# Block attention and two expert layers: host-side layouts, 64x64 attention products, and a list scheduler for the first part

## The chip, the cores and the metric

The kernel runs on one core of a Trainium2 chip. The metric is the device time of one execution in microseconds (us), as the median of several runs. Traces come from one profiled execution.

## What is computed

Eight batches of eight heads hold 576 tokens of 64 features. Attention works inside blocks of 64 tokens (9 blocks per sequence), so each head and block has a 64x64 score matrix. Its output, 4608 tokens by 512 features, goes through two dense layers in a row.

```
scores = q_c @ k_c.T / 8              # per block of 64 tokens
out    = softmax(scores) @ v_c        # -> x: 4608 x 512
h      = x @ w_in                     # 512 -> 1024
ln     = layernorm(h * softmax(h)) * g_ln
x      = ln @ w_out                   # 1024 -> 512
h2     = x @ w2_in                    # 512 -> 2048
y      = silu(h2) @ w2_out            # 2048 -> 512
```

q, k, v and g_ln are float32; the four weight matrices arrive as float64.

## The kernel before

There are three parts. The **first part** takes 36 tiles of 128 tokens through attention, `moe_in` (x @ w_in), the layer norm, and the transposes that the next product needs; every four tiles form a block of 512 tokens, whose `moe_out` (ln @ w_out) is done in four column groups. The result goes to HBM as `y1d`. The **second part** (`product`, L582) multiplies by `w2_in` with seven products in place of eight (Strassen's scheme), the **third** (`out_product`, L704) does the same with `w2_out`.

A dense product takes three passes of float32r matmuls (`PASSES`): high part by high part, high by low, low by high. So each operand is split into two float32r parts: ScalarE copies the high part (L384), VectorE subtracts for the low part (L393).

The four stages of a tile in the first part, with the lines that matter:

- `load_qk` and `load_v` fetch q, k and v straight from the inputs' own layout, two tiles at a time, in pieces of 64 or 128 KB (L279, L291, L302): 264 DMAs for q and k. `qk_transpose` turns q and k: on TensorE for the first six tiles (L313, with three ScalarE copies), on VectorE after that (L325, L328).
- `scores` (L336): eight float32 matmuls of 128 rows, 64 columns and 128 moving columns; k sits in a block-diagonal tile `kT` whose other half is zero, so half of the array's rows multiply zeros. `softmax_a` and `softmax_b` (L343 to L358) use VectorE, ScalarE and GpSimd. `attn_transpose` (L364) turns the weights, `attn_copy` (L370, two ScalarE copies of 64 partitions) puts them into the block-diagonal `pT`, and `attn_pv` (L378) is again eight matmuls of 128 moving columns. Each of these float32 matmuls shows as two records in the trace.
- `moe_in` (L409) is 24 matmuls of 512 columns, `ln_max` to `ln_norm` (L414 to L445) the layer norm. The scaling at its end runs on VectorE (L445) from the seventh tile on. PSUM holds one `h`, so the next tile's `moe_in` waits for L426.
- `ln_transpose` (L454, four transposes for each half) and `ln_split`; then `moe_out` (L468), 24 matmuls for each tile's share, and `y_store`.

Beside the tiles, `conv_load`, `conv_a`, `conv_b` and `conv_c` convert the weights from float64 in pieces of 128x512 (L159, L162, L176, L187, L203 or L209, and the split at L219, L221). There are 8 pieces of `w_in`, 8 of `w_out`, 16 of `w2_in` (followed by `w2_mix`, which writes sums of pieces to HBM). Odd pieces of the first sixteen are converted on GpSimd in part (L184, L207), even ones on VectorE; low parts are made on GpSimd (L221).

The order on every engine is fixed when the program is built: `Plan.at` gives each step a time, `Plan.run` emits in order of these times, and an engine runs its instructions in that order. In the first part the times are `T[t] = 14.3 t - 46.7` plus offsets; for the first 13 or so tiles a table of times (`LEAD`) replaces them.

PSUM's eight banks are: scores `S` 1, `K` 1, `px` 2 (`pp` and `xp`), `tr` 1, `y` 1, `h` 2. SBUF holds one `e`, one `pT`, one `xs` and two `u`.

Of the kernel before, what the change touches and what calls it, by code (L numbers as in the profile page):

```python
# [9 lines left out]
F32 = mybir.dt.float32  # L10
F32R = mybir.dt.float32r
# [13 lines left out]
class Plan:  # L25

    def __init__(self, lead):
        self.items = []
        self.lead = lead

    def at(self, when, fn, *args):
        lead = self.lead.get((fn.__name__, *(a for a in args if isinstance(a, int))))
        when = [x / 100 for x in lead] if lead else [when] if isinstance(when, float) else when
        self.items.append((when, fn, args))
# [11 lines left out]

@with_exitstack
def chunk_attention_moe_moe(ctx: ExitStack, tc: tile.TileContext, q, k, v, w_in, w_out, g_ln, w2_in, w2_out, out):
    nc = tc.nc
    B, H, S, D = q.shape
    NT, DM = out.shape
    F1 = w_in.shape[1]
    F2 = w2_in.shape[1]
    CH = 64
    HP = H // 2
# [4 lines left out]
    NG = 3  # L64
# [3 lines left out]
    CW = 512  # L68

# [26 lines left out]

    kT = sb.tile([128, 2 * HP, 2, CH], F32, tag="kT", name="kT")
    nc.vector.memset(kT, 0.0)
    pT = sb.tile([128, HP, 2, 2, CH], F32, tag="pT", name="pT")
    nc.vector.memset(pT, 0.0)  # L100


# [5 lines left out]
    for i in range(2 * KD):  # L108
        kk, c = i % KD, i // KD * CW

        heads = [(4 * (kk // 2) + 2 * g + kk % 2) * D for g in range(2)]
        pieces.append(("wi", kk, c, [w_in[r:r + D, c:c + CW] for r in heads], 1))
    for m in range(KD):
        for a in range(2):
            src = w_out[a * 512:(a + 1) * 512, m * 128:(m + 1) * 128].rearrange("(k p) f -> p k f", p=128)
            pieces.append(("wo", m, a, src, 4))
    for j in range(K2 // 2):
        for f in (j, j + K2 // 2):
            pieces.append(("w2", f, 0, w2_in[:, f * 128:(f + 1) * 128].rearrange("(k p) f -> p k f", p=128), KD))
    for j in range(K2 // 2):  # L120
        for f in (j, j + K2 // 2):
            pieces.append(("w2", f, 1, w2_out[f * 128:(f + 1) * 128, :], 1))
    conv, whole = {}, {}

    def cut(ap, n):
        return ap.rearrange("p (a f) -> p a f", a=n) if n > 1 else ap
# [3 lines left out]
    def conv_load(i):  # L130
        kind, _, _, src, n = pieces[i]
        wide = w_in.dtype != F32
        if kind == "wi":
# [5 lines left out]
        for r, part in ((slice(0, 64), src[0]), (slice(64, 128), src[1])) if kind == "wi" else ((slice(0, 128), src),):  # L139
            nc.sync.dma_start(out=cut((st if wide else st[:, 0:CW])[r], n), in_=part.bitcast(I32) if wide else part)  # L140
        conv[i] = [st, None]
# [24 lines left out]
    def conv_b(i, on=DVE):  # L166
# [11 lines left out]
        if on == POOL:  # L178
            yield
            L = st[:, 0:CW].bitcast(F32)  # L180
            nc.scalar.activation(out=M, in_=cv[:, 1, :], func=AF.Copy, scale=2.0 ** -20)
            nc.scalar.activation(out=L, in_=low, func=AF.Copy, scale=2.0 ** -52)
            yield
            nc.gpsimd.tensor_tensor(out=M, in0=M, in1=L, op=ALU.add)  # L184
        else:
            yield
            nc.vector.scalar_tensor_tensor(out=M, in0=low, scalar=2.0 ** -32, in1=cv[:, 1, :], op0=ALU.mult, op1=ALU.add)  # L187

    def conv_c(i, on=DVE):

        kind, x, y, _, n = pieces[i]
        st, cv = conv.pop(i)
        if st.dtype == F32:
            F, P, unit = st[:, 0:CW] if cv is None else cv[:, 1, :].bitcast(F32), None, 1.0
        else:
            F, P = cv[:, 1, :].bitcast(F32), cv[:, 0, :].bitcast(F32)
            unit = 1.0 if on == POOL else 2.0 ** -20
        if kind == "wo":
            for j in range(4):
                s = slice(128 * j, 128 * j + 128)  # L200
                gain = gsb[:, 4 * y + j:4 * y + j + 1] if unit == 1.0 else gsb20[:, 4 * y + j:4 * y + j + 1]
                if P is not None:
                    nc.vector.scalar_tensor_tensor(out=F[:, s], in0=F[:, s], scalar=gain, in1=P[:, s], op0=ALU.mult, op1=ALU.mult)  # L203
                else:
                    nc.vector.tensor_scalar(out=F[:, s], in0=F[:, s], scalar1=gain, scalar2=None, op0=ALU.mult)
        elif P is not None and on == POOL:
            nc.gpsimd.tensor_tensor(out=F, in0=F, in1=P, op=ALU.mult)  # L207
        elif P is not None:
            nc.vector.scalar_tensor_tensor(out=F, in0=F, scalar=unit, in1=P, op0=ALU.mult, op1=ALU.mult)  # L209
# [4 lines left out]
        if kind == "wi":  # L214
            hi, lo = (w[x][:, y:y + CW] for w in wi)
        else:
            hi, lo = (w[y][:, :, 128 * x:128 * x + 128] for w in wo)
            F = cut(F, 4)
# [48 lines left out]
    raw, val, qk, att, pvs, x_t = {}, {}, {}, {}, {}, {}  # L267

    def load_qk(g):
        c, b0 = g // 2, g % 2 * 4  # L270
        qr = sb.tile([128, 4, HP, 2, 32], F32, tag="qr", name="qr", bufs=2)
        kr = sb.tile([128, 4, HP, 2, 32], F32, tag="kr", name="kr", bufs=2)
        raw[g] = [qr, kr]
        if g < NG:

            for tt in range(2):
                for src, dst in ((q, qr), (k, kr)):
                    for c2 in range(2):
                        nc.sync.dma_start(  # L279
                            out=dst.rearrange("p (tt x) hp tb j -> p tt (x hp tb j)", tt=2)[64 * c2:64 * c2 + 64, tt].rearrange("p (h d) -> p h d", d=D),  # L280
                            in_=src[b0 + 2 * tt + c2, :, c * CH:(c + 1) * CH, :].rearrange("h s d -> s h d"),
                        )
                    yield
            return
        for src, dst in ((q, qr), (k, kr)):
            rows = src[b0:b0 + 4].rearrange("b (hp h2) s d -> h2 s (b hp) d", h2=2)
            for h2 in range(2):
                for e in range(2):
                    for tb in range(2):
                        p0, s0 = 64 * h2 + 32 * e, c * CH + 32 * tb  # L290
                        nc.sync.dma_start(  # L291
                            out=dst[p0:p0 + 32, :, :, tb, :].rearrange("p b hp j -> p (b hp) j"),
# [799 lines left out]
```

## Time and profile before

| | us |
|---|---|
| median of 3 runs | 1323.95 |
| lowest, highest | 1322.4, 1325.07 |
| span of the profiled execution | 1327.0 |
| start of the second part's first matmul | 590.93 |
| from the first tile's last `moe_in` record to the first `moe_out` | 48.98 to 101.27 |
| start of `moe_in` of the seventh and of the last tile | 115.73 and 549.02 |

For the profiled execution only the span is given, 3.05 us above the median. PE is the matrix engine (TensorE), PEld its weight loads, DVE VectorE, ACT ScalarE, POOL GpSimd, SP the engine that issues the DMAs. The clock of TensorE is given as a share of full speed (1.00 is 2.4 GHz, 0.50 is 1.2 GHz). A line number is that of the kernel before.

### The profile page before, as it was taken

The page shows a single profiled execution, that of the slowest core. Times are in us where ns is not written, and L with a number is a line of the kernel's source. Part 1 is how long each engine was busy: PE and PEld are TensorE (multiplying, and loading weights), DVE is VectorE, ACT ScalarE, POOL GpSimd, SP SyncE. Part 2 cuts the span into 40 slices and gives each one's busy share as a digit, 9 for nine tenths or more (in the row PEclk, how much of TensorE's full clock was granted, in tenths as well). Part 3 has the DMA queues.
Part 4 walks back from the last instruction along what each step waited for, and adds up shares of the span by engine and source line. Part 5 has one row for each costly group of instructions (what it writes and reads, how often), then busy time and mean ns, then how long its engine had stood idle before and what let it go on. Part 6 is the DMA issues. An engine that isn't in the chain of part 4 may idle for free. (4 is left out here: it accounts for less than half of the span.)

```text
span 1327.0 us, 22478 instructions
## 1 busy us (share of the span) xinstructions
PE 1266.0 (95%) x8400; PEld 1158.4 (87%) x8400; DVE 909.9 (69%) x1387; ACT 609.6 (46%) x991; POOL 558.8 (42%) x450
## 2 busy tenths in 40 slices
PE   3789999999999999999999999999999999999998
PEld 2578887887888888789899999999999999999998
DVE  7799777887888788524656656563678666666671
ACT  5677444544545545433435444443433343434341
POOL 4443113321312332321554446343137666667662
PEclk9989999999999999999999999999999999999999
DMA  9573456556545641769577655758993443443420
GB/s 205 93 139 74 91 112 155 130 107 165 140 104 144 155 115 64 273 235 297 168 229 237 211 183 187 240 166 278 354 331 119 139 149 111 138 148 113 136 92 29
DMA packets 330846, 217.51 MB, mean 164 GB/s; under 512 B 187248, under 2 KB 288624, under 8 KB 330736
## 3 DMA queue, kind: packets, MB, share of 16 engines
q1 hardware_dynamic: 330736, 216.07, 57.7%
q8 instruction: 66, 1.08, 0.3%
q14 instruction: 44, 0.36, 0.1%
HBM read 130.03 MB, written 85.98 MB: 163 GB/s over the span
## 5 line engine op out<-in xcount | busy, mean ns | idle before, releaser
L704 PE MATMUL h<-w2o,gs 128*128 128x256 f32 x2160 | 266.2, 284 | 2.5 <-DVE gs L697 2.0
L704 PEld LDWEIGHTS h<-w2o,gs 128*128 128x128 f32 x2160 | 262.7, 192 | 2.9 <-DVE gs L697 2.2
L582 PE MATMUL h<-y1s,w2t 128*128 128x384 f32 x1440 | 259.7, 335 | 1.4 <-ACT tmp L595 0.8
L582 PEld LDWEIGHTS h<-y1s,w2t 128*128 128x128 f32 x1440 | 251.3, 188 | 2.9 <-DVE tmp L599 1.5
L409 PE MATMUL h<-wi,xs 128*128 128x512 f32 x864 | 219.2, 403 | 6.6 <-DVE u L426 3.7
L468 PE MATMUL yp<-lnT,wo 128*128 128x512 f32 x864 | 211.9, 395 | 0.7 <-ACT ys L473 0.7
L409 PEld LDWEIGHTS h<-wi,xs 128*128 128x128 f32 x864 | 161.4, 192 | 45.8 <-ACT e L348 2.9
L468 PEld LDWEIGHTS yp<-lnT,wo 128*128 128x128 f32 x864 | 159.1, 188 | 38.5 <-issue 5.0
L695 ACT ACTIVATE gs<-g 128x1024 fp32r<-128x1024 f32 x117 | 123.6, 1059 | 140.5 <-PE h L704 74.8
L697 POOL TENSOR_TENSOR gs<-g,gs 128x1024 fp32r<-128x1024 f32 x50 | 138.1, 2764 | 49.4 <-ACT gs L695 44.3
L697 DVE TENSOR_TENSOR gs<-g,gs 128x1024 fp32r<-128x1024 f32 x67 | 116.7, 1746 | 31.2 <-ACT gs L695 30.3
L582 PE MATMUL hw<-y1s,w2t 128*128 128x384 f32 x576 | 109.9, 339 | 7.4 <-DVE tmp L613 7.4
L582 PEld LDWEIGHTS hw<-y1s,w2t 128*128 128x128 f32 x576 | 101.5, 189 | 9.3 <-DVE tmp L613 9.1
L704 PE MATMUL hw<-w2o,gs 128*128 128x256 f32 x864 | 108.7, 282 | 0.0
L704 PEld LDWEIGHTS hw<-w2o,gs 128*128 128x128 f32 x864 | 105.4, 191 | 0.0
L436 POOL TENSOR_TENSOR st<-st,nhalf 128x1 f32<-128x1 f32 x36 | 21.3, 592 | 177.9 <-DVE st L434 177.8
L239 POOL TENSOR_TENSOR cv<-cv 128x256 f32<-128x256 f32 x64 | 46.2, 741 | 90.7 <-DVE cv L209 89.4
L358 POOL TENSOR_TENSOR e<-e,sm 128x512 f32<-128x512 f32 x36 | 42.1, 1170 | 90.1 <-DVE sm L356 83.4
L393 DVE TENSOR_TENSOR lnT<-tp,lnT 128x512 fp32r<-128x512 f32 x72 | 49.4, 686 | 38.1 <-ACT lnT L384 37.4
L384 ACT ACTIVATE lnT<-tp 128x512 fp32r<-128x512 f32 x72 | 42.9, 596 | 61.8 <-PE tp L454 61.7
L684 POOL TENSOR_TENSOR g<-g,g0x 128x1024 f32<-128x1024 f32 x18 | 43.5, 2416 | 62.8 <-DVE gs L697 58.5
L615 ACT ACTIVATE tmp<-tmp 128x384 f32<-128x384 f32 x48 | 24.7, 528 | 90.3 <-DVE tmp L613 83.9
(116 smaller groups left out, 1805.4 us busy)
## 6 DMA issues: line engine op xcount, KB each, us to landing
gd<-tmp SPq DMA_DIRECT2D x192, 192.0 KB
g<-gd SPq DMA_DIRECT2D x72, 512.0 KB
w2d<-cv_m SPq DMA_DIRECT2D x56, 256.0 KB
w2t<-w2d SPq DMA_DIRECT2D x56, 256.0 KB
w2od<-y1s SPq DMA_DIRECT2D x56, 256.0 KB
w2o<-w2od SPq DMA_DIRECT2D x27, 512.0 KB
st_w<-in_moe_w_out_dram SPq DMA_DIRECT2D x24, 512.0 KB
vt<-in_v_dram SPq DMA_DIRECT2D x36, 256.0 KB
```

Source lines behind the costliest of these rows:

```text
L239: nc.gpsimd.tensor_tensor(out=out, in0=in0, in1=in1, op=op)
L358: nc.gpsimd.tensor_tensor(out=e, in0=e, in1=sm.to_broadcast([128, HP, 2, CH]), op=ALU.mult)
L384: nc.scalar.activation(out=hi, in_=src, func=AF.Copy)
L393: nc.vector.tensor_tensor(out=lo, in0=src, in1=hi.bitcast(F32), op=ALU.subtract)
L409: nc.tensor.matmul(h_t[t][:, n, :], xs[:, a, kk, :], wi[b][kk][:, n * 512:(n + 1) * 512], start=(kk == 0 and i == 0), stop=(kk == KD - 1 a ...
L468: nc.tensor.matmul(yps[b, m], wo[a][f // 4][:, f % 4, 128 * m:128 * (m + 1)], lnT[b][c][:, f, :], start=(f == 0 and i == 0), stop=(f == K1 ...
L582: nc.tensor.matmul(acc, w[:, a, kk, :], t[:, i, c, :], start=start and kk == 0 and n == 0, stop=kk == 1 and n == 2, skip_group_check=not s ...
L615: nc.scalar.activation(out=c, in_=c, func=AF.Silu)
L684: on.tensor_tensor(out=out, in0=in0, in1=in1, op=op_)
L695: nc.scalar.activation(out=dst[:, 0], in_=src, func=AF.Copy)
L697: (nc.gpsimd if o > (3 if v > 1 else 5) else nc.vector).tensor_tensor(out=dst[:, 1], in0=src, in1=dst[:, 0].bitcast(F32), op=ALU.subtract)
L704: nc.tensor.matmul(acc, g[:, a, f, :], wo2[o, f][:, c, :], start=start and f == 0 and i == 0, stop=f == NF - 1 and i == 2, skip_group_chec ...
```

## The change

The host hands over q and k, v, `w_in` and `w2_in` already in the order in which a tile or a piece is loaded; no value is changed. For every tile there is one DMA of 512 KB for q and k together and one of 256 KB for v, with rows of 4 and 2 KB; every weight piece is one contiguous DMA. q and k come with the features on the partitions, so `qk_transpose` and the block-diagonal tiles `kT` and `pT` go.

`attend(t)` does the output product of tile t and the scores of tile t + 2 together: 16 and 16 matmuls of 64 rows, 64 columns and 64 moving columns, ordered so that four neighbours use the four quarters of the array. Its PSUM tile `sx` (two banks, one buffer) holds both results. The softmax (`weigh`) is the same arithmetic with one ScalarE copy of 128 partitions at its end.

Conversion pieces run on VectorE alone (the GpSimd form is gone); the low part of the 8 `w_in` pieces moves from GpSimd to VectorE, that of the 8 `w_out` pieces stays on GpSimd. `w_out` pieces are whole rows, so their scaling is one instruction of 512 columns instead of four of 128. The scaling at the end of the layer norm runs on ScalarE for all tiles, with one more small GpSimd product; `x_split` makes its low part on VectorE for all tiles.

Buffers: `e`, `pT`, `xs`, `tr` and `y` two, `u` four, `qk` three; `sx` takes the place of `S`, `K` and `px`. In the second part the accumulators use `tr`, `sx`, `y` and `h`, and the places into which the second and third parts' weights are loaded change with the buffers.

The order of the first part comes from `Steps.solve`, a list scheduler: each step has an engine, a length, what it needs and frees, and each engine takes the ready step with the earliest due time. The due times come from `NOMINAL` (12.6 us a tile after the tenth). It holds no step back until a time, so loads and conversions of `w2_in` run as early as their places allow.

The core of the diff (cut):

```diff
+            for e in engines:
+                if free_at[e] > now + 1e-9:
+                    continue
+                st = min((st for st in ready[e] if all(places[p] > 0 for p in st["take"])), key=lambda st: st["rank"], default=None)
+                if st is None:
+                    continue
+                ready[e].remove(st)
+                for place in st["take"]:
+                    places[place] -= 1
+                start = now
+                if e == "PE":
+                    start += 0.1 * (mode != st["mode"])
+                    mode = st["mode"]
+                if st["port"]:
+                    start = max(start, port["POOL" if e == "DVE" else "DVE"])
+                    port[e] = start + st["length"]
+                st["start"], st["end"] = start, start + st["length"]
+                free_at[e] = st["end"]
...
+def stage_one(T, way_out, w2_from, tiles=36, per=4, ahead=2):
+
+    step = Steps(dict(S=1, X=1, tr=2, y=2, h=1, u=4, xs=2, e=2, pT=2, qk=3, v=2, ln=2, ys=2, st=2, cv=2, cvs=2))
+    op = step.op
+    dma = lambda kb, **more: ("DMA", kb * 1024 / 300e3, more)
+    sp = lambda n=1, **more: ("SP", 0.62 * n, more)
+    for t in range(tiles):
...
+    for t in range(-ahead, tiles):
+        n = t + ahead
+        old, new = t >= 0, n < tiles
+        op("attend", (t,), ("PE", 0.07 + 0.49 * (old + new), dict(mode=1, need=[("p", t), ("v", t)] * old + [("qk", n)] * new, take=["S"] * new + ["X"] * old,
+                                                                  free=["pT", "v"] * old + ["qk"] * new, give=[("s", n)] * new)),
+           *[("ACT", 0.59, dict(take=["xs"])), ("DVE", 0.69, dict(give=[("xs", t)], free=["X"], due=T[t] - 0.5))] * old)
+        if new:
+            op("weigh", (n,), ("DVE", 1.38, dict(need=[("s", n)], take=["e"], free=["S"])), ("ACT", 0.63, {}), ("DVE", 1.05, {}), ("POOL", 1.17, {}),
+               ("PE", 0.45, dict(take=["tr"])), ("ACT", 0.59, dict(take=["pT"], free=["tr", "e"], give=[("p", n)])))
+    wi = [[("w", 4 * n + kk) for kk in range(4)] for n in range(2)]
+    wo = [("w", i) for i in range(8, 16)]
+    for t in range(tiles):
+        b, tt = divmod(t, per)
+        x = T[t]
+        op("moe_in", (t,), ("PE", 2.73, dict(need=wi[0] + [("xs", t)], take=["h"], due=x + 2.73)),
+           ("PE", 2.73, dict(need=wi[1], free=["xs"], give=[("h", t)], due=x + 5.5)))
+        op("norm", (t,), ("DVE", 1.23, dict(need=[("h", t)])), ("ACT", 1.3, dict(take=["u"])),
+           ("DVE", 1.83, dict(free=["h"], due=x + gap - 0.5)), ("ACT", 1.34, {}), ("DVE", 0.15, {}), ("POOL", 0.85, {}),
+           ("ACT", 1.12, dict(give=[("u", t)])))
+        y = x + way_out + gap
+        for half in range(2):
+            op("turn_ln", (t, half), ("PE", 0.45, dict(need=[("u", t)], take=["tr"] + ["ln"] * (tt == 0 and half == 0))), ("ACT", 0.6, {}),
+               ("DVE", 0.69, dict(free=["tr"] + ["u"] * half, give=[("l", b, half, tt)], due=y + 3 * half)))
+    for b in range(tiles // per):
+        for m in range(4):
+            t = per * b + per + m
+            due = (T[t] if t < tiles else T[-1] + gap + 5.5 * (t - tiles)) + way_out + 5
+            op("moe_out", (b, m), ("PE", 2.73, dict(need=wo + [("l", b, 0, i) for i in range(per)] + [("o", b, m - 1)] * (m > 0), take=["y"], due=due + 2.7)),
+               ("PE", 2.73, dict(need=[("l", b, 1, i) for i in range(per)], free=["ln"] * (m == 3), give=[("o", b, m)], due=due + 5.5)),
+               ("ACT", 0.6, dict(take=["ys"], free=["y"])), sp(), dma(256, free=["ys"]))
+    return step
...
-        nc.gpsimd.tensor_tensor(out=lo, in0=F, in1=hi.bitcast(F32), op=ALU.subtract)
+        (nc.vector if kind == "wi" else nc.gpsimd).tensor_tensor(out=lo, in0=F, in1=hi.bitcast(F32), op=ALU.subtract)
...
+    def load_qk(t):
+        qk_t[t] = sb.tile([128, 2, 2, HP, CH], F32, tag="qk", name="qk", bufs=3)
+        nc.sync.dma_start(out=qk_t[t], in_=qk[t])
+
+    def load_v(t):
+        val[t] = sb.tile([128, 2, HP, D], F32, tag="vt", name="vt", bufs=2)
+        nc.sync.dma_start(out=val[t], in_=v[t])
+
+    def attend(t):
+
+        n = t + AHEAD
+        sx = ps.tile([128, 2, 512], F32, tag="sx", name="sx")
+        if t >= 0:
+            pT, vt = p_t.pop(t), val.pop(t)
+            for a in range(2):
+                for c in range(2):
+                    for h2 in range(2):
+                        for g in range(2):
+                            r, hp = slice(64 * h2, 64 * h2 + 64), 2 * a + g
+                            x0 = 256 + 128 * a + 64 * c
+                            nc.tensor.matmul(sx[64 * g:64 * g + 64, h2, x0:x0 + 64], vt[r, c, hp, :], pT[r, hp, c, :], start=True, stop=True)
+        if n < TT:
+            qT, kT = (qk_t[n][:, i] for i in range(2))
+            for hp in range(HP):
+                for h2 in range(2):
+                    for c in range(2):
+                        r = slice(64 * h2, 64 * h2 + 64)
+                        nc.tensor.matmul(sx[64 * c:64 * c + 64, h2, 64 * hp:64 * hp + 64], qT[r, c, hp, :], kT[r, c, hp, :], start=True, stop=True)
+            sx_t[n] = sx[:, :, 0:256].rearrange("p h (a k) -> p h a k", k=CH)
+        if t >= 0:
+            yield
+            xs = x_t[t] = sb.tile([128, 2, 2, 256], F32R, tag="xs", name="xs", bufs=2)
+            yield from split(xs[:, 0], xs[:, 1], sx[:, :, 256:512])
...
+        nc.gpsimd.tensor_tensor(out=rs, in0=rs, in1=nhalf, op=ALU.pow)
+        nc.gpsimd.tensor_tensor(out=off, in0=nmu, in1=rs, op=ALU.mult)
+        yield
+        nc.scalar.activation(out=u, in_=u, func=AF.Identity, bias=off, scale=rs)
...
-            if at_ == "w":
-                if "w" not in bank:
-                    bank["w"] = ps.tile([128, 2, 512], F32, tag="h", name="hw")
-                bank[u, at_] = bank["w"][:, u % 2, 0:n]
+            if at_ in "wy":
+                if at_ not in bank:
+                    bank[at_] = ps.tile([128, 2, 512], F32, tag={"w": "h", "y": "sx"}[at_], name="h" + at_)
+                bank[u, at_] = bank[at_][:, u % 2, 0:n]
             else:
-                tag, bufs = {"x": ("px", 2), "y": ("SK"[u % 2], 1), "v": (("tr", "y")[u % 2], 1)}[at_]
-                bank[u, at_] = ps.tile([128, 512], F32, tag=tag, name="h2", bufs=bufs)[:, 0:n]
...
-    plan = Plan(LEAD)
+    step = stage_one(NOMINAL, WAY_OUT, W2_FROM, TT, BT, AHEAD)
+    fns = dict(load_qk=load_qk, load_v=load_v, convert=convert, w2_mix=w2_mix, attend=attend, weigh=weigh,
+               moe_in=moe_in, norm=norm, turn_ln=turn_ln, moe_out=moe_out)
+    plan = Plan()
     at = plan.at
-    L = 14.3
+    at(-1.0, gain_load)
+    at(5.0, gain_scale)
+    for (name, *args), when in step.solve().items():
+        at(when, fns[name], *args)
...
+FIRST = [-14.8, 16.57, 3, 3.46, 8.49, 9.95, 15.13, 10.28, 17.44, 8.76]
+NOMINAL = [sum(FIRST[:t + 1]) + 12.6 * max(0, t + 1 - len(FIRST)) for t in range(36)]
+WAY_OUT = 20.65
+W2_FROM = 12
...
+    qk = _np.stack([heads(x).transpose(0, 3, 5, 1, 2, 4) for x in "qk"], axis=3).reshape(36, 128, 2, 2, 4, 64)
+    data = dict(qk=qk, v=heads("v").transpose(0, 3, 4, 1, 2, 5).reshape(36, 128, 2, 4, 64))
+    data["w_in"] = wide["moe_w_in"].reshape(2, 2, 2, 64, 2, 512).transpose(4, 2, 0, 1, 3, 5).reshape(2, 4, 128, 512)
+    data["w_out"] = wide["moe_w_out"]
```

## Rows read from the trace of the kernel before

**Rows 1.** The page: span and busy time of each engine.
```profile
span 1327.0 us, 22478 instructions
PE 1266.0 (95%) x8400; PEld 1158.4 (87%) x8400; DVE 909.9 (69%) x1387; ACT 609.6 (46%) x991; POOL 558.8 (42%) x450
```

**Rows 2.** Busy time by stage (window, length, busy and count, clock, DMA, GB/s).
```profile
0.00:48.98 48.98, 22.06 (x121) 15.70 (x121) 38.76 (x47) 25.70 (x43) 26.84 (x27) 1.00 1.07 193
48.98:101.27 52.29, 44.64 (x310) 36.10 (x309) 44.24 (x92) 40.44 (x68) 20.50 (x21) 0.90 0.52 96
115.73:549.02 433.29, 427.85 (x2672) 349.33 (x2670) 345.93 (x648) 221.91 (x381) 116.65 (x128) 1.00 0.53 125
549.02:590.93 41.91, 38.36 (x173) 30.71 (x173) 15.10 (x21) 12.75 (x21) 11.22 (x7) 1.00 0.79 294
590.93:1327.00 736.07, 718.62 (x5041) 714.64 (x5039) 452.24 (x553) 299.38 (x462) 376.87 (x261) 0.99 0.58 185
```

**Rows 3.** Timeline of PE, one steady tile (start, length, line, tile, count).
```profile
382.81 1.15 PE L378 MATMUL xp<-pT,vt 128*64 128x128 f32 x16
383.74 1.09 PE L336 MATMUL S<-kT,qT 128*64 128x128 f32 x16
384.76 3.02 PE L468 MATMUL yp<-lnT,wo 128*128 128x512 f32 x12
...
397.53 1.15 PE L378 MATMUL xp<-pT,vt 128*64 128x128 f32 x16
```

**Rows 4.** Line 378's instructions alone, first 0.03 us of one group.
```profile
382.80:382.83 0.03, 0.02 (x2) 0.02 (x2) 1.00 0.60 94
```

**Rows 5.** Waits in the first part (engine line, releaser: total, times, longest).
```profile
PE pp L364 <- POOL e L358: 6.9, 12, 2.3
PE h L409 <- DVE u L426: 3.7, 4, 2.4
```

**Rows 6.** VectorE groups, first 590 us (busy, mean ns).
```profile
L343 DVE TENSOR_REDUCE mx<-S 128x8 f32<-128x512 f32 x36 | 24.5, 682 | 0.0
L414 DVE TENSOR_REDUCE st<-h 128x1 f32<-128x1024 f32 x36 | 44.1, 1224 | 11.9 <-PE h L409 11.1
L426 DVE SCALAR_TENSOR_TENSOR u<-u,st,h 128x1024 f32<-128x1024 f32 x36 | 46.1, 1281 | 1.4
L424 DVE TENSOR_SCALAR st<-st 128x1 f32<-128x1 f32 x36 | 5.5, 152 | 16.8 <-ACT u L417 16.8
L203 DVE SCALAR_TENSOR_TENSOR cv<-cv,gsb 128x128 f32<-128x128 f32 x32 | 9.3, 356 | 0.1
L445 DVE TENSOR_SCALAR u<-u,st 128x1024 f32<-128x1024 f32 x30 | 25.9, 862 | 19.6 <-POOL st L436 19.5
```

**Rows 7.** Timeline of VectorE at the start: weight pieces being converted.
```profile
5.76 0.43 DVE L159 TENSOR_SCALAR cv_e<-st_e 128x512 int32<-128x512 int32 x1 [2.75 <-DMA st_e<-in_moe_w_in_dram]
6.10 0.42 DVE L162 TENSOR_SCALAR cv_e<-st_e 128x512 int32<-128x512 int32 x1
7.04 0.69 DVE L176 SCALAR_TENSOR_TENSOR cv_e<-st_e,cv_e 128x512 int32<-128x512 int32 x1 [0.52 <-ACT cv_e L164]
7.65 0.68 DVE L187 SCALAR_TENSOR_TENSOR cv_e<-st_e,cv_e 128x512 f32<-128x512 uint32 x1
...
15.07 1.49 DVE L162 TENSOR_SCALAR cv<-st_e 128x512 int32<-128x512 int32 x1
```

**Rows 8.** DMA of the first 60 us.
```profile
DMA packets 23379, 9.87 MB, mean 165 GB/s; under 512 B 21328, under 2 KB 22352, under 8 KB 23376
```

**Rows 9.** Timeline of PE: the fifth tile and the first output product.
```profile
89.62 5.46 PE L409 MATMUL h<-wi,xs 128*128 128x512 f32 x12 [2.38 <-DVE u L426]
...
101.27 3.03 PE L468 MATMUL yp<-lnT,wo 128*128 128x512 f32 x12
```

**Rows 10.** The two halves of moe_in of the fifth tile (columns as rows 2).
```profile
89.62:94.87 5.25, 5.25 (x12) 3.99 (x13) 5.17 (x12) 1.93 (x4) 2.66 (x4) 0.50 0.77 136
95.94:98.79 2.85, 2.85 (x15) 2.29 (x14) 1.91 (x6) 2.83 (x5) 0.00 (x0) 1.00 0.65 169
```

More of the change, by code (lines that the diff above doesn't have):

```diff
@@ L51, in chunk_attention_moe_moe @@
 @with_exitstack
-def chunk_attention_moe_moe(ctx: ExitStack, tc: tile.TileContext, q, k, v, w_in, w_out, g_ln, w2_in, w2_out, out):
+def chunk_attention_moe_moe(ctx: ExitStack, tc: tile.TileContext, qk, v, w_in, w_out, g_ln, w2_in, w2_out, out):
     nc = tc.nc
-    B, H, S, D = q.shape
+    B, HP, CH, D = 8, 4, 64, 64
     NT, DM = out.shape
[L56 to L59, printed above, removed]
+    F1 = w_in.shape[0] * w_in.shape[3]
+    F2 = w2_in.shape[0] * 128
     KD = DM // 128
@@ L195, in conv_c @@
         else:
-            F, P = cv[:, 1, :].bitcast(F32), cv[:, 0, :].bitcast(F32)
-            unit = 1.0 if on == POOL else 2.0 ** -20
+            F, P, unit = cv[:, 1, :].bitcast(F32), cv[:, 0, :].bitcast(F32), gsb20
         if kind == "wo":
[L199 to L207, printed above, removed]
+            gain = unit[:, x:x + 1]
@@ L264, in gain_scale @@
         nc.vector.tensor_scalar(out=gsb20, in0=gsb, scalar1=2.0 ** -20, scalar2=None, op0=ALU.mult)
[L267 to L292, printed above, removed]
-                            in_=rows[h2, s0:s0 + 32, :, 32 * e:32 * e + 32],
-                        )
-                    yield
@@ L395, in x_split @@
-    def x_split(t, on=DVE):
-        xs = sb.tile([128, 2, HP, 128], F32R, tag="xs", name="xs")
-        x_t[t] = xs
-        yield from split(xs[:, 0], xs[:, 1], pvs.pop(t), on)
-    h_t, ln, lnT, trp, yps = {}, {}, {}, {}, {}
-    def moe_in(t, n):
-        xs = x_t[t]
-        if n == 0:
-            h_t[t] = ps.tile([128, 2, 512], F32, tag="h", name="h")
-        for kk in range(KD):
-            for i, (a, b) in enumerate(PASSES):
-                nc.tensor.matmul(h_t[t][:, n, :], xs[:, a, kk, :], wi[b][kk][:, n * 512:(n + 1) * 512],
-                                 start=(kk == 0 and i == 0), stop=(kk == KD - 1 and i == 2))
@@ new lines, in chunk_attention_moe_moe, with moe_in @@
+    h_t, ln, lnT = {}, {}, {}
+    def moe_in(t):
+        xs = x_t.pop(t)
+        h_t[t] = ps.tile([128, 2, 512], F32, tag="h", name="h")
+        for n in range(2):
+            if n:
+                yield
+            for kk in range(KD):
+                for i, (a, b) in enumerate(PASSES):
+                    nc.tensor.matmul(h_t[t][:, n, :], xs[:, a, kk // 2, 128 * (kk % 2):128 * (kk % 2) + 128], wi[b][kk][:, n * 512:(n + 1) * 512],
+                                     start=(kk == 0 and i == 0), stop=(kk == KD - 1 and i == 2))
@@ L830, in chunk_attention_moe_moe @@
             at([when + (8.8 if tag == "wo" else 0.01) * i + (2.2 if tag == "wo" else 0.001) * k for k in range(n + 1)], t_load, tag, BUFS.get(tag, 2), n)
[L831 removed]
+    x = max(step.last("w2_mix"), step.last("attend", engine="PE") - 2.0)
+    at(x, raw_places, 0)
     for i in range(4):
[L833 to L835 removed]
+        at(x + 0.1 + 0.01 * i, raw_load, 0, i)
+    at(x + 10.0, raw_t, 0, 0)
+    at(x + 12.0, raw_t, 0, 1)
     at(XO + 0.2, s_places, 0)
```

515 lines of the change are left out of this document (181 added, 334 removed), and 44 rows, old and new, of the table LEAD.

## The prediction

> **What bounds the kernel now.** I read the page first [rows 1]: TensorE is busy for 95% of the span, no other engine for more than 69%. A share over three parts hides where each is short, so the windows by stage come next [rows 2]. From 590.93 on, the second and third parts take 736.07 us; the change touches there only the names of buffers. In the first part the stretch from the seventh to the last tile, 433.29 us for 29 tiles, is 14.94 us a tile. TensorE is busy for 427.85 of it, so it idles 5.44 us, 0.19 a tile; VectorE has 345.93. This stretch is TensorE's. Ahead of it the picture turns round: up to 48.98 us TensorE has 22.06 us of work, VectorE 38.76. From there to the first output product VectorE works 44.24 of 52.29. So the start is VectorE's, and what it must convert before all weights stand decides it.
>
> The timeline of one steady tile [rows 3] prices what the change replaces. The old `attn_pv` takes 0.93 us from its start to that of the next group, the old `scores` 1.02: 1.95 us of a tile that in this place takes 14.72. Each is 16 records, 61 ns apart on average.
>
> **The attention products.** 32 records become 64 (each float32 matmul is two), each with half the moving columns. If four quarters of the array work at once where two column halves do now, the group costs 1.95 x 2 x 1/2 x 1/2 = 0.98 us. Nothing before uses a quarter, so I bound it. Below: 0.98, since no row shows a column that costs less. Above: 64 records at today's 61 ns are 3.9 us, 1.95 more than now. I take 0.98, because 61 ns is the spacing of streams of 128 columns, and where a group starts with two records for different halves the trace shows both in a window of 0.03 us [rows 4]: records for free parts of the array are not held to 61 ns. Gain 0.97 us a tile.
>
> The other TensorE work of a tile, two dense products and three groups of transposes, stays as it is.
>
> **The small idle of the steady tiles.** The two waits of TensorE that stand out are for the softmax product on GpSimd, 6.9 us in 12 places, and for the release of `h`, 3.7 us in 4 [rows 5], partly at the start. Two `e`, two `pT`, two `xs`, four `u` and two more PSUM places give the first kind slack. I take the 0.19 us as gone; its bound on the other side is an idle as large as now. So 29 x (0.97 + 0.19) = 33.6 us.
>
> **The start.** The transposes of q and k leave TensorE, which has time there, so that is worth nothing by itself. VectorE gets more: the GpSimd form of the odd pieces goes, and so does the GpSimd low part of `w_in`. One `w_in` piece is 0.43 + 0.42 + 0.69 + 0.68 [rows 7], one more scaling and one subtraction of 512 columns at 0.68 each: 3.6 us, 28.6 for eight. A `w_out` piece is 2.9: its scaling is one instruction of about 0.68 instead of four of 0.356 [rows 6]; 23.2 for eight. A tile is six passes of 512 columns at 0.68, one of 1.22 and one of 1.28, and seven small ones of about 0.15 [rows 6]: 7.7 us. Before the first output product VectorE needs sixteen pieces, four whole tiles (30.8) and the softmax of two more (2 x 2.4): from its first piece at 5.76 us that is 5.76 + 28.6 + 23.2 + 30.8 + 4.8 = 93.2 us if it never waits. Today the first output product starts at 101.27 [rows 9]. So 8 us are won at best by this sum. If VectorE waits as long as now (95.5 us from 5.76 to 101.27, less 83.0 busy [rows 2], is 12.5), it is 105.7, 4 later. The durations overlap a little at their ends (the second pass starts 0.34 us after a first one of 0.43 [rows 7]), so there is slack in the sum, and I take the 8. What speaks for little waiting: a pass that needs 0.42 alone took 1.49 beside GpSimd work [rows 7], and GpSimd, busy for 47.3 us up to 101.27 [rows 2], loses its share of the conversions. The loads should not be what is late: of the 23379 packets of the first 60 us, 21328 are under 512 B [rows 8], and rows of 2 and 4 KB replace the pieces of q, k and v among them.
>
> **What costs nothing.** The last scaling of the layer norm, 0.86 us on VectorE [rows 6], goes to ScalarE, which has 221.91 us of work in 433.29 [rows 2]; with the added GpSimd product the chain of a tile gets about 1 us longer. Four `u` hide it; without them the output product of the tile would be later by that. The 264 small DMAs for q and k become 36 on SP's queue, which lets the loads of weights and the stores of `y1d` behind them go earlier. The conversions of `w2_in` have no start time in the scheduler, so their passes, the `w2_mix` sums and its 56 DMAs run early, in VectorE's and GpSimd's free time; behind each waits at most one step of a tile for one pass (0.69). At the seam TensorE has the last block's four output products, two halves of up to 3.02 each [rows 3], so up to 24 us, while the operands of the second part are loaded and split, as now. The end of the first part idles 3.55 us [rows 2], and I leave that. The second and third parts: zero.
>
> **Sum.** 33.6 + 8 = 42 us. The profiled execution would go from 1327.0 to 1285, and the median, 3 us below its span, from 1324 to 1282.
>
> **Rivals.** *Issue paces the small matmuls.* The four quarters may stand ready while instructions can't come fast enough. If only the columns halve and no more records run at once than now, 64 records cost 64 x 30.5 ns = 1.95 us, no gain. Then 29 x 0.19 + 8 = 13.5 remain: 1310. For it: no run of 64 such records is in this trace. Against it: rows 4. The Trainium skill has a rule here (TensorE: Matmul & The Clock Gate, the section "Wait — 56ns, not 53.3ns?"): matmuls never start less than about 25 ns apart, however few columns they have. By it a group would be an estimated 1.6 us and the sum about 1300. The two records of rows 4 do not keep to it, but two are not sixty-four.
>
> *The start gives back.* VectorE waits for landings and hand-overs as now (+4), and passes still stretch beside GpSimd: 16 pieces with two passes each that gain 1.07 us (1.49 less 0.42) are 34 us; with none to half of that, the first output product comes 4 to 21 us later than now. With the steady gain kept: 1324 - 33.6 + 4 = 1294 to 1311. For it: +16 us of VectorE passes by the list above. Against: GpSimd's smaller share.
>
> *Slower: `h` released late.* There is one `h`, and its release (L426) stands in VectorE's fixed order behind whatever the scheduler put there with its own lengths, conversions of `w2_in` among them. The fifth tile shows the price [rows 9, 10]: `moe_in` waited 2.38 us for L426, the granted clock fell to 0.50 (the 1.2 GHz level), and the first half took 5.25 us instead of 2.85. One such stall costs 2.38 + 2.40 = 4.8 us. It decides from the ninth on: 42 / 4.8 = 9 of 36 tiles. At every second tile, 18 x 4.8 = 86 us: 1324 - 42 + 86 = 1368. For it: a fixed order made from lengths that the chip does not keep. Against: of a tile's 13.8 us TensorE has some 8 beside the two halves of `moe_in` at 2.85 [rows 10], and the chain to the release is two VectorE passes of 1.22 and 1.28 [rows 6] with one ScalarE pass between them.
>
> **Chances.** Forecast 0.62, issue 0.20, start 0.09, late `h` 0.09. The median of the likeliest case is 1282. Low end 1266: VectorE's overlaps give some 5 us more at the start and the seams and the end could lose their idle of a few us each. High end 1312: the issue case and the start case whole. The slow rival stays outside. About 0.2% (2.6 us) is what a measurement of this kernel can tell from no change; the edge of the issue case falls in there, 0.03. Slower is the late `h`, 0.09; faster 0.88.
>
> **What would show it.** In the changed trace the 64 records of a steady `attend` should take about 1 us from their first start to the next dense group; near 2 us is the issue rival. The steady period should be 13.8 us a tile with no idle of TensorE over 0.1. The first output product should start near 93 us with VectorE full until then; 105 or more is the start rival. Stalls of `moe_in` on L426's successor with a granted clock of 0.50 past the sixth tile would show the slow one. I am wrong if the gain sits in the second or third part, or if the period does not fall.

## The result and the profile after

The changed kernel takes 1286.79 us (median of 4 runs, 1284.61 to 1288.99), the kernel before 1323.41 beside it: a ratio of 0.9718, 95% interval 0.9696 to 0.9740. The profiled execution took 1286.21 us, with a span of 1284.4. The spans are 42.6 us apart, the medians 36.6. A span is about 1.8 us shorter than the time of its execution (1286.21 and 1284.4 here), so the profiled execution of before took an estimated 1328.8 us, some 5 above its median, and that of after 0.6 less than its own. The 36.6 is what the change is worth; the 42.6 is what these two traces can be asked about.

The windows by stage of the changed kernel, cut at the same events as [rows 2] (seventh and last tile's `moe_in`, first product of the second part):

```profile
39.84:109.79 69.95, 54.59 (x646) 43.21 (x644) 60.53 (x120) 42.79 (x70) 18.08 (x22) 0.89 0.35 119
109.79:508.31 398.52, 398.52 (x3484) 327.08 (x3485) 254.58 (x516) 227.80 (x368) 118.86 (x153) 1.00 0.38 133
508.31:548.89 40.58, 40.58 (x189) 33.48 (x188) 12.59 (x17) 14.84 (x23) 11.49 (x8) 1.00 0.78 287
548.89:1284.40 735.51, 718.25 (x5041) 713.58 (x5039) 448.47 (x553) 299.42 (x462) 379.23 (x261) 0.99 0.57 184
```

The 42.6 us come off piece by piece against [rows 2]: up to the seventh tile 115.73 - 109.79 = 5.9; seventh to last tile 433.29 - 398.52 = 34.8; the last tile and its products 41.91 - 40.58 = 1.3; the second and third parts 736.07 - 735.51 = 0.6. In the second window TensorE's busy time equals the window: no idle is left, and a tile takes 13.74 us instead of 14.94.

The timeline of PE, one steady tile, answers to [rows 3]:

```profile
392.15 0.60 PE L500 MATMUL tp<-ident,u 128*128 128x128 f32 x4
392.68 0.69 PE L412 MATMUL sx<-pT,vt 64*64 64x64 f32 x32
393.20 0.65 PE L419 MATMUL sx<-qk 64*64 64x64 f32 x32
393.77 3.04 PE L511 MATMUL yp<-lnT,wo 128*128 128x512 f32 x12
...
406.36 0.69 PE L412 MATMUL sx<-pT,vt 64*64 64x64 f32 x32
```

Output product and scores take 0.52 + 0.57 = 1.09 us where they took 1.95. This tile takes 13.68.

The start, in the same timeline (it answers to [rows 9]), and two windows of it (columns as above, answering to [rows 10]):

```profile
84.75 7.33 PE L466 MATMUL h<-wi,xs 128*128 128x512 f32 x24 [3.97 <-DVE u L481]
...
96.87 8.65 PE L466 MATMUL h<-wi,xs 128*128 128x512 f32 x24 [2.68 <-DVE u L481]
...
109.79 5.77 PE L466 MATMUL h<-wi,xs 128*128 128x512 f32 x24 [1.40 <-DVE u L481]
115.40 2.88 PE L511 MATMUL yp<-lnT,wo 128*128 128x512 f32 x12
```

```profile
84.75:92.01 7.26, 7.26 (x25) 5.54 (x25) 6.77 (x13) 4.86 (x7) 3.31 (x5) 0.76 0.01 2
96.87:105.36 8.49, 8.49 (x24) 6.64 (x25) 5.78 (x12) 4.37 (x6) 3.40 (x4) 0.64 0.31 109
```

The fifth, sixth and seventh tiles wait for the release of `h` (L481, the old L426), and two of their `moe_in` run in part at the 1.2 GHz level (granted clock 0.76 and 0.64): 7.33 and 8.65 us instead of 5.77. The first output product starts at 115.40, 14 us later than before, behind seven `moe_in` instead of five.

VectorE up to there: the window from 5.76 us, where the prediction's sum starts, and two of its groups by line, up to 115.40.

```profile
5.76:115.40 109.64, 70.91 (x804) 55.80 (x797) 99.30 (x191) 59.24 (x96) 22.67 (x26) 0.89 0.45 164
```

```profile
L473 DVE TENSOR_REDUCE st<-h 128x1 f32<-128x1024 f32 x6 | 7.3, 1222 | 6.6 <-PE h L466 6.6
L429 DVE TENSOR_REDUCE mx<-sx 128x8 f32<-128x512 f32 x9 | 6.1, 678 | 3.4 <-PE sx L419 2.9 <-ACT xs L451 0.5
```

VectorE (the third pair) is busy for 99.30 of 109.64 us. It begins six layer norms (L473) and nine softmaxes (L429) before the first output product.

### The profile page after: what moved, and what is told of

It reads as the page before. It is cut to its first block, busy times and chain, and to the rows that moved or that the text cites. A ratio compares the mean times of both kernels' runs of the same rounds, so it can differ in the third digit from the quotient of the medians.

```text
span 1284.4 us, 24171 instructions
## 1 busy us (share of the span) xinstructions
PE 1223.3 (95%) x9504; PEld 1126.0 (88%) x9504; DVE 809.5 (63%) x1267; ACT 599.5 (47%) x945; POOL 530.8 (41%) x454
## 4 chain that ended last, share of the span: by engine, by line
PE 86%; DVE 7%; DMA 2%; issue 2%; POOL 1%; ACT 0%; SPq 0%; DVEq 0%; POOLq 0%; ACTq 0%
PE yp L511 16%; PE h L466 15%; PE h L745 11%; PE h L623 9%; PE hw L745 8%; PE hy L745 8%; PE hy L623 7%; PE hw L623 6%; PE tp L500 2%; PE sx L412 1%; PE pp L444 1%; PE sx L419 1%; DMA w2od<-y1s 1%; DMA st_w<-in_w_out_dram 1%; DVE cv L304 1%
## 5 line engine op out<-in xcount | busy, mean ns | idle before, releaser
L466 PEld LDWEIGHTS h<-wi,xs 128*128 128x128 f32 x864 | 165.7, 196 | 48.4 <-issue 7.1
L511 PEld LDWEIGHTS yp<-lnT,wo 128*128 128x128 f32 x864 | 157.6, 188 | 33.6
L623 PE MATMUL h<-y1s,w2t 128*128 128x384 f32 x864 | 162.2, 335 | 0.0
L745 PE MATMUL h<-w2o,gs 128*128 128x256 f32 x1296 | 161.5, 280 | 0.0
L745 PEld LDWEIGHTS h<-w2o,gs 128*128 128x128 f32 x1296 | 156.6, 189 | 0.0
L623 PEld LDWEIGHTS h<-y1s,w2t 128*128 128x128 f32 x864 | 151.6, 188 | 0.1
L745 PE MATMUL hy<-w2o,gs 128*128 128x256 f32 x864 | 110.8, 285 | 2.3 <-DVE ob L758 2.3
L473 DVE TENSOR_REDUCE st<-h 128x1 f32<-128x1024 f32 x36 | 44.0, 1223 | 109.2 <-PE h L466 109.2
L623 PE MATMUL hy<-y1s,w2t 128*128 128x384 f32 x576 | 109.0, 337 | 2.5 <-DVE tmp L640 2.5
L745 PEld LDWEIGHTS hy<-w2o,gs 128*128 128x128 f32 x864 | 107.3, 193 | 2.4 <-ACT gs L736 2.4
L623 PEld LDWEIGHTS hy<-y1s,w2t 128*128 128x128 f32 x576 | 100.6, 188 | 4.5 <-DVE tmp L640 4.3
```

What stands on the lines that cost most here:

```text
L466: nc.tensor.matmul(h_t[t][:, n, :], xs[:, a, kk // 2, 128 * (kk % 2):128 * (kk % 2) + 128], wi[b][kk][:, n * 512:(n + 1) * 512], start=(kk ...
L473: nc.vector.tensor_reduce(out=mx, in_=h, axis=AX.XY, op=ALU.max, negate=True)
L511: nc.tensor.matmul(yp, wo[a][f // 4][:, f % 4, 128 * m:128 * (m + 1)], lnT[b][c][:, f, :], start=(f == 0 and i == 0), stop=(f == K1 - 1 an ...
L623: nc.tensor.matmul(acc, w[:, a, kk, :], t[:, i, c, :], start=start and kk == 0 and n == 0, stop=kk == 1 and n == 2, skip_group_check=not s ...
L745: nc.tensor.matmul(acc, g[:, a, f, :], wo2[o, f][:, c, :], start=start and f == 0 and i == 0, stop=f == NF - 1 and i == 2, skip_group_chec ...
```

## The experiments

Each is the changed kernel with one edit. "First part ends" is the start of the second part's first matmul, 548.89 in the changed kernel.

### What sets the time of the attention matmuls

By quarter:

```diff
-            for a in range(2):
-                for c in range(2):
-                    for h2 in range(2):
-                        for g in range(2):
+            for h2 in range(2):
+                for g in range(2):
+                    for a in range(2):
+                        for c in range(2):
```

(and the scores' loops likewise, `h2` and `c` outside `hp`)

> The changed kernel with the attention matmuls ordered by quarter of the array: the four matmuls of one quarter come one behind the other, then the next quarter's. In the changed kernel a steady attend takes 0.52 + 0.57 = 1.09 us, the first part ends at 548.89 us and the span is 1284.4. Theory A (each quarter works off its own queue, so the order of issue matters little): attend stays within 0.1 us of 1.09, span within 4 us of 1284. Rival (only neighbours for different quarters overlap): eight records of one quarter run one after the other, at about 56 ns (half of the 109 ns between two records of one half before) some 0.45 us per quarter and 1.8 per group, so attend takes up to 3.6 us, 2.5 more; 36 tiles make +90 us, span near 1374.

One run took 1337.03 us, span 1335.2, first part to 600.05: 13 us slower than before the change. The timeline of PE, a steady `attend`, and the window from the seventh to the last tile:

```profile
416.35 1.36 PE L412 MATMUL sx<-pT,vt 64*64 64x64 f32 x29
...
417.73 1.31 PE L419 MATMUL sx<-qk 64*64 64x64 f32 x29
418.97 1.20 PE L511 MATMUL yp<-lnT,wo 128*128 128x512 f32 x4
```

```profile
119.77:559.47 439.70, 439.70 (x3486) 368.47 (x3485) 256.43 (x516) 228.44 (x369) 118.06 (x153) 1.00 0.37 121
```

`attend` takes 418.97 - 416.35 = 2.62 us, 41 ns a record, for the same matmuls that take 1.09 when neighbours use different quarters. A tile takes 439.70 / 29 = 15.16, still without idle: `attend` is 1.53 us longer and the tile 1.42, so TensorE time in a steady tile is paid almost in full. The records of one quarter, counted in windows that start just before the first of them (L412 alone; the number behind the first x is that of matmul records):

```profile
416.34:416.49 0.15, 0.14 (x2) 0.14 (x3) 1.00 0.00 0
416.34:416.55 0.21, 0.20 (x3) 0.20 (x4) 1.00 0.00 0
416.34:416.61 0.27, 0.26 (x4) 0.26 (x5) 1.00 0.00 0
```

One quarter takes a record every 0.06 us. Eight quarters' turns of eight records would be 64 x 0.06 = 3.8 us, near the rival's 3.6; 2.62 is between the two expectations: some overlap across quarters is left, far from all. The Trainium skill says that different tiles of the array "can execute LdWeights and Matmul in parallel" (TensorEngine Tiling (Array Packing), Key Properties). Here that holds only as far as the instruction order offers work for them.

Half columns, first with the two halves of a matmul as neighbours:

```diff
-  nc.tensor.matmul(sx[64*g:64*g+64, h2, x0:x0+64], vt[r, c, hp, :], pT[r, hp, c, :], ...)
+  for z in (0, 32):
+      nc.tensor.matmul(sx[64*g:64*g+64, h2, x0+z:x0+z+32], vt[r, c, hp, :], pT[r, hp, c, z:z+32], ...)
```

> The changed kernel with every attention matmul cut into two of 32 moving columns: 128 records instead of 64 for the same columns. Theory A (the columns streamed set the time of a group): attend stays near 1.09 us, span within 4 us of 1284. Rival (issue sets it, 1.09 us / 64 = 17 ns for a record): attend doubles to 2.2 us, 36 x 1.1 = +39 us, span near 1324.

1315.52 us (one run), first part to 580.52. An `attend` of 128 records took 2.05 us, the time that issue as the pace would give, but two neighbours then share a quarter, which the run before had shown to cost. So the same cut again with the loop over `z` outside the loops over quarters:

> The attention matmuls cut into two of 32 moving columns as in the run with half columns, but ordered so that four neighbours still use four different quarters (there, two neighbours shared one). 128 records took 2.05 us there, 16 ns each. If issue sets the pace: 2.05 us again, first part ends near 580.5. If the shared quarter of the neighbours was to blame and columns set the pace: near 1.1 us, first part ends near 549.

1316.90 us (one run), first part to 578.42. The timeline of PE and the same stretch as a window:

```profile
399.96 0.61 PE L499 MATMUL tp<-ident,u 128*128 128x128 f32 x4
400.50 1.14 PE L411 MATMUL sx<-pT,vt 64*64 64x32 f32 x64
401.45 1.11 PE L418 MATMUL sx<-qk 64*64 64x32 f32 x64
402.50 3.02 PE L510 MATMUL yp<-lnT,wo 128*128 128x512 f32 x12
```

```profile
400.50:402.50 2.00, 2.00 (x130) 1.96 (x129) 1.48 (x2) 0.60 (x1) 0.00 (x0) 0.95 0.03 8
```

2.00 us for 128 records with half the columns in each: nearly twice the time, as the issue theory had it. But the total doesn't tell issue from a fixed time of each quarter, and the starts of the records do. Counted as above, in the changed kernel (L412), in this run (L411), and in the kernel before (L378, two halves of 128 moving columns; it goes on from [rows 4]):

```profile
392.67:392.71 0.04, 0.03 (x4) 0.03 (x4) 1.00 0.00 0
392.67:392.82 0.15, 0.14 (x8) 0.14 (x12) 1.00 0.00 0
392.67:392.84 0.17, 0.16 (x8) 0.16 (x12) 1.00 0.00 0
392.67:392.88 0.21, 0.20 (x12) 0.20 (x16) 1.00 0.00 0
```

```profile
400.49:400.53 0.04, 0.03 (x4) 0.03 (x4) 0.95 0.00 0
400.49:400.61 0.12, 0.11 (x8) 0.11 (x8) 0.95 0.00 0
400.49:400.67 0.18, 0.17 (x12) 0.17 (x13) 0.95 0.00 0
```

```profile
382.80:383.07 0.27, 0.26 (x4) 0.26 (x6) 1.00 0.56 87
382.80:383.18 0.38, 0.37 (x6) 0.37 (x8) 1.00 0.52 81
```

Four records, one for each quarter, start within 0.04 us, then comes a pause until the next four. So records can be issued at 0.01 us each or less, and issue is not what sets the pace. What does is the quarter: it takes its next record about 0.06 us after the last one (here 401.45 - 400.50 = 0.95 us for 16 rounds, 59 ns), with 64 columns and with 32 alike, and by itself as among four (the run by quarter). A half took a record of 128 columns every 0.11 us. Between 128 and 64 columns the time of a record therefore falls almost by half, below 64 it doesn't fall; shorter records would gain nothing. Each record comes with a weight load of its own; whether the load or the matmul holds the 0.06 us was not tested.

The granted clock of this run's first part is recorded as 0.95, between its two levels; the 12 dense matmuls behind `attend` took 3.02 us, as long as at 1.00 (3.04 in the changed kernel). The page that the prediction weighed (the Trainium skill, TensorE: Matmul & The Clock Gate, "Wait — 56ns, not 53.3ns?") has about 25 ns as the least between starts; on four quarters in turn the trace shows four starts within 0.04 us, and 15.6 ns in the mean over the 128.

### Does the length of the rows in HBM matter?

```diff
-        nc.sync.dma_start(out=qk_t[t], in_=qk[t])
+        nc.sync.dma_start(out=qk_t[t].rearrange("p a b h s -> p (a b h) s"), in_=qk[t].rearrange("n p s -> p n s"))
```

(v likewise; the host's order is such that every run is 64 floats)

> The changed kernel with q, k and v laid out in HBM so that each load again consists of runs of 256 bytes (one DMA per tile as in the changed kernel, same bytes, same places in SBUF). Theory (the long rows only relieve the first 40 us): the steady period stays 13.7 us; the w_in pieces land later, and the second half of the first moe_in comes 0 to 5 us after 39.84; span 1284 to 1290. Rival (the layout carries a large part of the gain): the DMA engines fall behind in the steady part too, attend waits for qk or v, the period grows by 0.3 us or more, span over 1294.

1285.17 us (one run), first part to 549.04, second half of the first `moe_in` at 41.19. The DMA view of the first 60 us, of this run and then of the changed kernel:

```profile
DMA packets 24196, 10.81 MB, mean 180 GB/s; under 512 B 22912, under 2 KB 22912, under 8 KB 24192
```

```profile
DMA packets 4495, 11.07 MB, mean 184 GB/s; under 512 B 1422, under 2 KB 1422, under 8 KB 4491
```

Five times the packets, 1.3 us at the start, nothing at the end. The host's layout is worth what it lets the kernel leave out (the transposes, the zero halves), not the shape of its rows. The number of DMAs, one for each tile here as in the changed kernel, was not varied.

### What the doubled buffers are worth

All of them back to the counts of before:

```diff
-  step = Steps(dict(S=1, X=1, tr=2, y=2, h=1, u=4, xs=2, e=2, pT=2, ...))
+  step = Steps(dict(S=1, X=1, tr=2, y=2, h=1, u=2, xs=1, e=1, pT=1, ...))
```

(and `bufs` of the four tiles; the space goes to tiles that only the later parts use)

> The changed kernel with one e, one pT and one xs and two u as before the change, in the kernel and in the scheduler's list (the freed space is kept for the later parts under other names). Theory (the doubled buffers removed the idle of 0.19 us a tile): idle of TensorE of 0.2 us or more a tile returns, the period goes from 13.74 to 13.9 or more, the first part ends at 555 or later. Rival (the order alone removed it): the period stays within 0.05 us of 13.74.

1335.00 us (one run), first part to 599.17: slower than before the change, with the small attention matmuls in place. The window from the seventh to the last tile, and in it the group of `moe_in` among PE's groups by line:

```profile
123.22:558.61 435.39, 409.47 (x3458) 331.15 (x3456) 252.28 (x501) 223.19 (x362) 114.34 (x150) 0.96 0.35 121
```

```profile
L466 PE MATMUL h<-wi,xs 128*128 128x512 f32 x697 | 186.0, 418 | 14.1 <-DVE u L481 10.0 <-DVE st L487 3.0 <-ACT cv_m L375 1.1
```

25.9 us of idle in 29 tiles, most of it before `moe_in`, and a granted clock of 0.96: a tile takes 15.01. The start is 13.4 us longer too (123.22 against 109.79). Then two of the four alone:

> The changed kernel with one e and one pT (kernel and list), two xs and four u as in the change. If the softmax chain is what needs places (scores two tiles ahead, one e passed from VectorE through ScalarE, GpSimd and TensorE): the first part ends 15 us or more after 548.89, with idle of TensorE in the steady tiles before pp or sx. If xs carries the 50 us: within 8 us.

1315.02 us (one run), first part to 580.04, and the same window:

```profile
112.00:539.48 427.48, 411.05 (x3553) 334.20 (x3553) 259.66 (x519) 226.79 (x370) 116.47 (x153) 0.97 0.37 128
```

14.74 us a tile with 16.4 us of idle: 31 of the 50 us come with `e` and `pT`.

> The changed kernel with two u instead of four (kernel and list; the freed space is kept under another name). With one e, pT and xs and two u the first part ended at 599.17. If u carries a part of that (the longer chain through GpSimd and ScalarE holds its u longer): the first part ends 5 us or more after 548.89. If it is the attention chain's buffers alone: within 2 us.

1285.33 us (one run), first part to 549.00: two `u` are enough as long as the other buffers are doubled. What is left of the 50 us, 19, goes with the single `xs`, alone or together with the others; that was not run by itself. In these runs the scheduler solves its list for the smaller places, so what is shown is buffers and order together: with one place each, its order is worse than the written times of before.

### What sets the start

> The changed kernel with the low parts of the eight w_in pieces back on GpSimd, in the kernel and in the scheduler's list. Theory V (VectorE's work sets the start): 8 x 0.61 = 4.9 us leave VectorE ahead of the first tile, so the seventh tile's moe_in starts near 105 instead of 109.79 and the first part ends near 544. Rival H (from the third tile on the single h and the chain that releases it set the start): the second half of the first moe_in comes earlier than 39.84 us, but the end moves by less than 2 us from 548.89.

The edit is `low = ("POOL", 1.26, ...)` for all sixteen pieces in the list, and `nc.gpsimd` for all low parts. 1293.44 us (1293.33 to 1295.24), ratio 0.9772 (0.9750 to 0.9794): 7 us slower than the changed kernel. The timeline of PE has a part of the first tile's second half early, at 31.14, but it does not finish:

```profile
31.14 1.67 PE L466 MATMUL h<-wi,xs 128*128 128x512 f32 x6
37.80 0.79 PE L466 MATMUL h<-wi,xs 128*128 128x512 f32 x1 [4.99 <-ACT wi L333]
39.15 2.50 PE L466 MATMUL h<-wi,xs 128*128 128x512 f32 x5 [0.56 <-POOL wi L335]
```

The last pieces now wait for GpSimd, the seventh tile starts at 112.03 and the first part ends at 556.26. Theory V fails; H had the end unchanged and misses by 7.

> The changed kernel with two h in PSUM and one tr and one y in place of two each (kernel and scheduler). Theory H (the release of the single h sets tiles 3 to 7): the waits for it (0.42 + 3.97 + 2.68 + 1.40 = 8.5 us) and the half-clock matmuls behind them (7.33 + 8.65 against 2 x 5.75, 4.5 us) go, and the first part ends 8 to 13 us earlier, 536 to 541, unless one tr and one y bring stalls into the steady tiles. Theory V (VectorE's work sets the start): the end moves by less than 3 us.

The edit: `h=2, tr=1, y=1` in the list, `bufs` likewise. 1298.68 us (1298.44 to 1301.17), ratio 0.9816 (0.9796 to 0.9837). The timeline of PE, and the windows from the seventh tile on (to the thirteenth, then to the last):

```profile
98.59 0.66 PE L500 MATMUL tp<-ident,u 128*128 128x128 f32 x4 [2.19 <-DVE lnT L453]
99.00 3.01 PE L466 MATMUL h<-wi,xs 128*128 128x512 f32 x12
...
112.10 0.66 PE L500 MATMUL tp<-ident,u 128*128 128x128 f32 x4 [2.69 <-DVE lnT L453]
...
120.40 3.02 PE L511 MATMUL yp<-lnT,wo 128*128 128x512 f32 x12
```

```profile
99.00:197.99 98.99, 93.75 (x788) 75.25 (x786) 69.19 (x137) 56.02 (x90) 30.43 (x40) 0.98 0.39 130
197.99:519.20 321.21, 314.82 (x2790) 256.87 (x2789) 199.26 (x398) 180.15 (x291) 94.13 (x121) 1.00 0.37 129
```

The seventh tile starts at 99.00, 10.8 us earlier: the single `h` did hold the tiles of the start. But the one `tr` now stalls TensorE (2.19 and 2.69 before a transpose), the idle in the steady tiles is 6.4 us where it was none, and the first part ends at 562.72. Behind the seventh tile the run loses 24.6 us; the idle in the two windows, 5.2 and 6.4, is about half of that, the rest was not traced.

> The changed kernel with the due times of the first block's output products 60 us earlier, so that the scheduler converts w_out ahead of the tiles' work. Theory V (VectorE's total work sets the start, as the prediction had it): the first output product starts near 93 us instead of 115.40, tiles come later by as much, and the first part ends within 2 us of 548.89. Theory H (the h chain leaves TensorE idle because no output product can fill it): products fill the waits of 8.5 us and the clock stays up, and the first part ends 5 to 13 us earlier.

The edit is `- 60.0 * (b == 0)` on the due time. 1305.41 us (1302.63 to 1310.03), ratio 0.9854 (0.9814 to 0.9894). The first product starts at 107.23 instead of 115.40, not at 93; the first tile's `moe_in` starts at 36.95 instead of 22.17, the seventh's at 133.96, and the first part ends at 570.53. Both theories miss: weights ahead of tiles hold up the tiles by more than the earlier products give back.

> The changed kernel with even due times of 12.6 us a tile from the first on, in place of the ten written spacings. If the written spacings carry the start: the first part ends 4 us or more later than 548.89. If only the scheduler's ranks behind them matter: within 3 us.

`NOMINAL = [-14.8 + 12.6 * t for t in range(36)]`: 1291.64 us (1289.44 to 1293.46), ratio 0.9749 (0.9720 to 0.9777); the first part ends at 554.49. The ten written spacings are worth some 5 us: there is still a short table of times in the kernel.

> The changed kernel without the pass that adds the low words to the eight w_out pieces (in the list of the scheduler too); this leaves out part of the conversion of w_out. Theory V (VectorE's work sets the start): 8 x 0.61 = 4.9 us less VectorE work before the first output product, which starts 4 to 5 us before 115.40, and the first part ends 4 to 5 us before 548.89. Theory H (the chain through the single h sets tiles 3 to 7): the first product may come earlier, the end moves by less than 1.5 us.

```diff
+        if pieces[i][0] == "wo":
+            return
         nc.vector.scalar_tensor_tensor(out=M, in0=low, scalar=2.0 ** -32, ...)
```

The edit also shortens the pass to nothing in the list, which is solved anew. 1288.80 us (1283.59 to 1290.72), ratio 0.9713 (0.9672 to 0.9755): no gain. The seventh tile starts at 114.18 and the first part ends at 554.79, 5.9 us later. The timeline of PE shows the same kind of waits as in the changed kernel:

```profile
100.59 5.24 PE L470 MATMUL h<-wi,xs 128*128 128x512 f32 x12 [4.44 <-DVE u L485]
...
114.18 4.17 PE L470 MATMUL h<-wi,xs 128*128 128x512 f32 x12 [3.02 <-DVE u L485]
118.15 2.22 PE L515 MATMUL yp<-lnT,wo 128*128 128x512 f32 x7
```

The first product came at 118.15, not 4 us earlier. Two runs take work from VectorE and none gets faster. In both the list was solved anew and the order came out worse, and in the first GpSimd became late, so they don't show what VectorE's work alone is worth; they show that less of it is not enough. That the chain through `h` holds the tiles is shown by the run with two `h`; what would shorten the start as a whole stays open, since every other order or split that was run gave the time back elsewhere.

## Why the prediction was right, and where it was not

**The total.** 42 us were forecast between the profiled executions and 42.6 came; the medians moved by 36.6, to 1286.79 against 1282, inside 1266 to 1312. That the spans agree so closely is in part luck: the profiled execution of before was a long one, some 5 us over its median, and the forecast put the median 3 us below the span after the change too, where it stands 2.4 above.

**The attention products.** Forecast 0.98 us for the 64 records, measured 1.09. The reason was right, for the order in which the code interleaves them: four quarters work at once (by quarter it is 2.62 us), and with half the columns a record takes its part of the array 0.06 us instead of 0.11. The 0.11 us too little is a size: the sum halved the whole group, while 16 rounds of 0.06 are some 0.95 and the rest is the start and the end of the group, which didn't halve. The issue rival failed in its cause, since four records start within 0.04 us; its 30.5 ns a record compares with 17 in the mean. It was right in one thing that the forecast had not: halving the columns once more gains nothing.

**The steady tile.** Forecast 13.8, measured 13.74; 33.6 us forecast for the 29 tiles, 34.8 measured. The products gave 0.86 of the 1.20 us a tile, the visible idle 0.19; the other 0.15 was not traced.

**The small idle.** The step put 0.19 us a tile on the doubled buffers. That was the idle of the old order, not the price of the buffers under the new one: without them the list's order costs 50 us, more than the whole gain. Here the argument was too thin, and the result was right because the buffers came with the change. Four `u`, which the text had as a cover that must not go, are two too many.

**The start.** This is the step that failed. The sum over VectorE put the first product at 93.2; it came at 115.40, past the 105 that was to mean the start rival. Still the seventh tile starts 5.9 us earlier, where 8 were forecast. The sum had 87.4 us of VectorE work and no wait from 5.76 us on; the window shows 99.30 us of work and 10.3 of waiting. So the step went wrong twice. VectorE's work was added up as if nothing else ordered it, but the scheduler puts tiles ahead of `w_out`: six layer norms and nine softmaxes were begun before the first product, where the sum had four and six. And VectorE waits for those tiles, 6.6 us for `moe_in` alone (L473), as they run at the pace of the chain from `moe_in` through VectorE and ScalarE to the release of `h`. The start of the first product was a bad mark for progress.

**The slow rival.** Its mechanism is in the trace, before the first product only: waits for L481 of 3.97, 2.68 and 1.40 us, and the clock at half for part of two `moe_in`. It decides from nine on; in the steady tiles there are none. That TensorE then has output products to fill with is the likely reason; no run shows it by itself.

**The parts at nothing.** Loads, SP's queue, the longer chain of the layer norm and the seam cost nothing that shows: the last window lost its idle (3.55 to 0), and the later parts are 0.6 us apart.

## What to carry to other kernels

Ask of a scheduler not only what the order gains but how many places it needs: with single buffers the same list was slower than the times written by hand. Small matmuls on quarters of the array pay in full only if neighbours in program order use different quarters. Before you cut them shorter, look at the starts of the records of one quarter: here a record of 32 columns held its quarter as long as one of 64, so shorter records do not help. Take as mark of progress the event behind which the bounding engine never idles again, not the first product of a kind.

## What the hardware showed that was not expected

- Four records for the four quarters start within 0.04 us, but a quarter takes its next record only 0.06 us after the last, with 64 columns or 32. In turn, 128 records take 2.00 us (15.6 ns each); one quarter after the other, 64 take 2.62 (41 ns each).
- Runs of 256 bytes for q, k and v, 22912 short packets in the first 60 us instead of 1422, cost 1.3 us at the start and nothing in the total.
- A late release of `h` costs more than its wait: behind waits of 3.97 and 2.68 us the granted clock fell to 0.76 and 0.64 in the mean of the `moe_in`, which took 1.6 and 2.9 us more (7.33 and 8.65 against 5.77). Behind the wait of 1.40 it stayed at 1.00.
